# The first load of a decode kernel in two halves of 64 partitions, from two issuing engines

## The chip, the core and the metric

The kernel runs on one core of a Trainium2 chip. A core has four engines that compute (TensorE, VectorE, ScalarE, GpSimd), SyncE, which here issues transfers, and 16 DMA engines that carry data between the chip's main memory (HBM) and the core's on-chip memory of 128 partitions (SBUF). SyncE and ScalarE each have a queue of transfers of their own. The metric is the device time of one execution in microseconds (us); the kernel before takes 691.82 us, the median of three runs.

## What is computed

One decode step: attention of one token with grouped heads over a cache of 32,768 positions, and beside it a gated feed-forward block, mixed by a scalar gate. All in float32.

```python
Hq, Hkv, Sk, Dh, D, F = 32, 8, 32768, 128, 512, 1792
g = sigmoid((x * gate_w).sum(-1, keepdims=True))
q = (x @ wq).reshape(1, 1, Hq, Dh).transpose(0, 2, 1, 3)
scores = einsum("bhqd,bhkd->bhqk", q, repeat(k_cache, 4)) * Dh ** -0.5
o = einsum("bhqk,bhkd->bhqd", softmax(scores), repeat(v_cache, 4))
a = o.transpose(0, 2, 1, 3).reshape(1, 1, Hq * Dh) @ wo
b = (silu(x @ w1) * (x @ w3)) @ w2
out = g * a + (1 - g) * b
```

The caches are 8 heads of 16.8 MB each for k and for v, 268 MB of the 296 MB that are read. wq and wo have 8.39 MB each, w1, w3 and w2 3.67 MB each.

## The kernel before

Three buffers of 128 partitions by 16,384 floats, `ra`, `rb` and `rc`, 8.39 MB each, take all large transfers in turn. All of these are issued by SyncE, in one fixed order, written out by hand at lines 34 and 131 to 165; each issue is preceded by a wait on a semaphore that says that the buffer's last reader is done. Transfers of SyncE's queue are carried in the order of issue.

The start: lines 30 to 34 issue wq into `rc` (semaphore `l_q`), and w1 and w3 side by side into `rb` (`l_w1`, `l_w3`). For wq each of the 128 partitions takes four rows of the matrix, which follow each other in HBM: one run of 65,536 B. Then all engines meet at a barrier (line 38). SyncE goes on with the two halves of the first k tile into `ra` (131, 132), and then waits (133) until TensorE has done the second of two passes over `rb` (`c_e`) before it issues the next k tile into `rb` (134). ScalarE issues three small transfers from its own queue: x, 2 KB (168), gate_w, eight runs of 256 B (169), and zeros to the output (175). Both loads add to the semaphore `l_x`.

The first computation: VectorE (192, 194) and TensorE (200) wait for `l_x`. From x TensorE makes `xp`, x laid over the partitions, and a sum for the gate (209). At line 210 it waits for `l_q` and then multiplies by wq (215). VectorE transposes the result (227), ScalarE copies it in 16 pieces into `winraw` (231), and GpSimd puts it into the weights' window (271). TensorE meanwhile waits for w1 and w3 and does the two passes of the feed-forward block (247 to 250, in `ff_rows`, line 242); ScalarE (254) and VectorE (256 to 261) make of them the hidden row `htp`, which is kept to the end. ScalarE waits ahead of that for the zeros' landing (252).

The loop: for each of the eight heads VectorE transposes the k tiles in place (355), TensorE multiplies them by the query (284) and, a head later, v by the probabilities (298); ScalarE takes the exponentials. At the end wo comes into `rc` in two halves (434 waits for each), and w2 into `ra` in five pieces (441, 451).

Of the kernel before, what the change touches and what calls it, by code (L numbers as in the profile page):

```python
# [9 lines left out]
P = 128  # L10
# [14 lines left out]
@with_exitstack  # L25
def kernel(ctx, tc, x, k_cache, v_cache, wq, wo, w1, w3, w2, gate_w, out):
    nc = tc.nc
    rb, rc = (nc.alloc_sbuf_tensor(n, [P, 16384], F32).ap() for n in ("rb", "rc"))
    l_q, l_w1, l_w3 = (nc.alloc_semaphore(n) for n in ("l_q", "l_w1", "l_w3"))
    loads = [(rc, wq, l_q)]  # L30
    n = w1.shape[0] * w1.shape[1] // P
    loads += [(rb[:, i * n:(i + 1) * n], w, sem) for i, (w, sem) in enumerate(((w1, l_w1), (w3, l_w3)))]
    for to, w, sem in loads:
        i = nc.sync.dma_start(to, w.rearrange("(p c) n -> p (c n)", p=P)).then_inc(sem, 16)

        tc.no_tile_sem_insts.add(i.ins.name)
    tc.close()
    tc.compile()
    _program(nc, rb, rc, l_q, l_w1, l_w3, x, k_cache, v_cache, wq, wo, w1, w3, w2, gate_w, out)


def _program(nc, rb, rc, l_q, l_w1, l_w3, x, k_cache, v_cache, wq, wo, w1, w3, w2, gate_w, out):
    pe, dve, act, pool, sp = nc.tensor, nc.vector, nc.scalar, nc.gpsimd, nc.sync
# [119 lines left out]
    for i in range(2):  # L163
        e = slice(i * D // 2, (i + 1) * D // 2)
# [42 lines left out]
    dve.tensor_copy(xp[:, :, 0], mc[:, NC:2 * NC]).then_inc(t_x, 1)  # L207
    take(t_x, 2)
    n_gate = c_q.by(pe.matmul(mc[:, 0:1], ones[0:1], gsm[0:1], start=True, stop=True))
    pe.wait_ge(l_q, 16)  # L210
    for c in range(NC):
        for b in range(2):
            for j in range(4):
# [225 lines left out]
    for k in range(W2[1]):  # L439
        t = k % 4  # L440
        i = pe.matmul(  # L441
            acc[32 * t:32 * t + 32, :], htp[:, k, :], w2t[:, k, :], start=False, stop=(k >= W2[1] - 4),
            skip_group_check=True,
        )
# [65 lines left out]
```

## Time and profile before

| | us |
|---|---|
| median of three runs | 691.82 |
| lowest and highest run | 691.80, 691.91 |
| span of the profiled execution, first to last instruction | 690.5 |
| TensorE matmul busy in it | 380.2 (55%) |
| VectorE busy | 307.0 (44%) |
| ScalarE busy | 41.7 (6%) |

The profiled execution's own time is given as its span alone; the median lies 1.3 us above it. A span leaves out what lies ahead of the first instruction and behind the last.

A row of the timeline gives the start and the duration in us, the engine (a name that ends in q is the sequencer, which issues), the line, the operation, what is written and read, the count, and in brackets the idle time before it and what ended it. A row of the DMA issues gives what goes where, the issuing queue, the count, and the median time from issue to landing. The line of GB/s divides the span, or a window of it, into 40 equal slices and counts a packet's bytes in the slice in which it starts. Queue q1 is SyncE's, q10 ScalarE's.

### The profile page before, as it was taken

The page shows a single profiled execution, that of the slowest core. Times are in us where ns is not written, and L with a number is a line of the kernel's source. Part 1 is how long each engine was busy: PE and PEld are TensorE (multiplying, and loading weights), DVE is VectorE, ACT ScalarE, POOL GpSimd, SP SyncE. Part 2 cuts the span into 40 slices and gives each one's busy share as a digit, 9 for nine tenths or more (in the row PEclk, how much of TensorE's full clock was granted, in tenths as well). Part 3 has the DMA queues.
Part 4 walks back from the last instruction along what each step waited for, and adds up shares of the span by engine and source line. Part 5 has one row for each costly group of instructions (what it writes and reads, how often), then busy time and mean ns, then how long its engine had stood idle before and what let it go on. Part 6 is the DMA issues. An engine that isn't in the chain of part 4 may idle for free. (4 is left out here: it accounts for less than half of the span.)

```text
span 690.5 us, 6710 instructions
## 1 busy us (share of the span) xinstructions
PE 380.2 (55%) x2946; PEld 107.8 (16%) x2946; DVE 307.0 (44%) x194; ACT 41.7 (6%) x111; POOL 7.1 (1%) x41
## 2 busy tenths in 40 slices
PE   1737256466463744567563735457463734466567
PEld 1200011103010121103020211103010211103122
DVE  1019378291725537091725447091815446191000
ACT  0020011002000010002000010002000010002000
POOL 0000000000000000000000000000000000000000
PEclk9975587879685876768577967778676966768678
DMA  9999999999999999999999999999999999999997
GB/s 410 400 434 455 425 430 430 448 440 429 426 429 437 425 437 444 437 429 425 433 433 433 444 440 429 425 429 437 429 444 440 433 425 429 437 425 437 441 417 318
DMA packets 6222, 296.35 MB, mean 429 GB/s; under 512 B 707, under 2 KB 963, under 8 KB 1094
## 3 DMA queue, kind: packets, MB, share of 16 engines
q1 hardware_dynamic: 6192, 296.23, 99.3%
q8 instruction: 6, 0.10, 0.1%
q14 instruction: 2, 0.02, 0.0%
q10 hardware_dynamic: 22, 0.01, 0.0%
HBM read 296.23 MB, written 0.00 MB: 429 GB/s over the span
## 5 line engine op out<-in xcount | busy, mean ns | idle before, releaser
L355 DVE STREAM_TRANSPOSE rb<-rb 128x2048 f32<-128x2048 f32 x64 | 141.8, 2274 | 150.3 <-DVEq L125 150.3
L284 PE MATMUL psum<-rb,winbuf 128*32 128x512 f32 x512 | 96.7, 836 | 122.9 <-PEq L125 122.9
L355 DVE STREAM_TRANSPOSE ra<-ra 128x2048 f32<-128x2048 f32 x64 | 141.4, 2276 | 43.0 <-DVEq L125 43.0
L298 PE MATMUL psum<-rc,prob 128*32 128x512 f32 x896 | 112.8, 660 | 41.3 <-PEq L125 41.3
L284 PE MATMUL psum<-ra,winbuf 128*32 128x512 f32 x512 | 87.5, 782 | 83.8 <-PEq L125 83.8
L298 PEld LDWEIGHTS psum<-rc,prob 128*32 128x32 f32 x896 | 33.6, 121 | 117.0 <-issue 116.8
L379 DVE TENSOR_REDUCE mx<-psum 128x4 f32<-128x1024 f32 x8 | 9.8, 1225 | 82.7 <-DVEq L125 82.7
L284 PEld LDWEIGHTS psum<-rb,winbuf 128*32 128x32 f32 x512 | 13.5, 125 | 202.7 <-issue 202.7
L393 ACT COPY sbuf<-psum 128x512 f32<-128x512 f32 x16 | 9.9, 618 | 478.0 <-PE psum L284 478.0
L284 PEld LDWEIGHTS psum<-ra,winbuf 128*32 128x32 f32 x512 | 14.9, 122 | 149.3 <-issue 149.3
L399 ACT ACTIVATE prob<-psum,nm 128x256 f32<-128x256 f32 x32 | 18.9, 695 | 39.3 <-DVE nm L387 39.3
L308 PE MATMUL psum<-ident,sbuf 128*64 128x64 f32 x512 | 16.7, 223 | 0.8 <-PEq L125 0.8
L308 PEld LDWEIGHTS psum<-ident,sbuf 128*64 128x64 f32 x512 | 15.6, 138 | 7.6 <-issue 7.6
L360 DVE SCALAR_TENSOR_TENSOR otall<-psum,gate,recip 128x4 f32 (+1 forms) x8 | 1.7, 214 | 32.8 <-DVEq L125 32.8
L298 PE MATMUL psum<-rb,prob 128*32 128x512 f32 x64 | 8.5, 690 | 9.7 <-DMA rb<-in_A_v_cache_dram 9.7
L215 PE MATMUL psum<-rc,xp 128*32 128x512 f32 x64 | 9.8, 782 | 4.7 <-DMA rc<-in_A_wq_dram 4.7
L434 PE MATMUL psum<-rc,oq 128*32 128x512 f32 x64 | 10.7, 829 | 2.6 <-DMA rc<-in_A_wo_dram 2.2
L271 POOL COPY winbuf<-winraw 32x16 f32<-32x16 f32 x32 | 6.1, 191 | 535.4 <-PE psum L284 499.7
L242 PE MATMUL psum<-rb,xp 128*32 128x448 f32 x64 | 8.6, 690 | 5.4 <-DMA rb<-in_B_w_dram 5.4
L298 PE MATMUL psum<-ra,prob 128*32 128x512 f32 x64 | 9.6, 770 | 3.3 <-DMA ra<-in_A_v_cache_dram 3.3
L200 PE MATMUL psum<-ones,ob 1*128 1x1 f32 x8 | 2.0, 370 | 15.2 <-DMA prob<-in_gate_w_dram 15.2
L318 PE MATMUL psum<-fold,ob 128*128 128x4 f32 x64 | 8.4, 255 | 0.8 <-PEq L125 0.8
(62 smaller groups left out, 79.0 us busy)
## 6 DMA issues: line engine op xcount, KB each, us to landing
ra<-in_A_k_cache_dram SPq DMA_DIRECT2D x2, 4096.0 KB, 52.6
rc<-in_A_wo_dram SPq DMA_DIRECT2D x2, 4096.0 KB, 45.5
rb<-in_B_w_dram SPq DMA_DIRECT2D x2, 3584.0 KB, 34.7
ra<-in_B_w_dram SPq DMA_DIRECT2D x1, 1792.0 KB, 33.4
ra<-in_B_w_dram SPq DMA_DIRECT2D x1, 1024.0 KB, 35.5
ra<-in_B_w_dram SPq DMA_DIRECT2D x1, 512.0 KB, 36.3
ra<-in_B_w_dram SPq DMA_DIRECT2D x2, 128.0 KB, 36.0
rc<-in_A_v_cache_dram SPq DMA_DIRECT2D x14, 30.4
```

The source lines that it names most:

```text
L215: m = pe.matmul(pq[b][32 * j:32 * j + 32, :], xp[:, c, :], rc[:, o:o + REP * DH], start=(c == 0), stop=(c == NC - 1),)
L242: i = pe.matmul(ps[32 * j:32 * j + 32, 0:FJ], xp[:, c, :], rb[:, o:o + FJ], start=(c == 0), stop=(c == NC - 1))
L271: pool.tensor_copy(winbuf[32 * r:32 * r + 32, 16:144].rearrange("p (c k) -> p c k", k=32)[:, :, 4 * r:4 * r + REP], winraw[32 * r:32 * r + ...
L284: i = pe.matmul(s_ps[m][32 * g:32 * g + 32, :], winbuf[:, w:w + 32], region.rearrange("p (n c i) -> p c n i", c=4, i=32)[:, c, n:n + 16], ...
L298: i = pe.matmul(o_ps[32 * t:32 * t + 32, :], prob[:, w:w + 32], region[:, n * DH:(n + 4) * DH], start=(r == 0 and g == 0 and f == 0), stop ...
L308: i = pe.matmul(pf[64 * s:64 * s + 64, 64 * a:64 * a + 64], sbuf[:, a].rearrange("p i m -> p (i m)"), ident.rearrange("p (gf r s q) -> p s ...
L318: i = pe.matmul(mb[:, 0:REP], ob[:, b * P:(b + 1) * P], fold[:, 4 * b:4 * b + 4], start=(b == 0), stop=(b == 3))
L355: dve.transpose(part[:, c], part[:, c]).then_inc(t_tr, 1)
L379: dve.tensor_reduce(mx, pf.rearrange("p (a q) -> p q a", q=REP), axis=AX.X, op=ALU.max).then_inc(t_mx, 1)
L393: act.copy(sbuf[:, :, :, m], s_ps[m].rearrange("p (n i) -> p n i", i=32)).then_inc(t_ev, 1)
L399: act.activation(prob[:, 0:1024].rearrange("p (a n q) -> p n a q", a=16, q=REP)[:, :, :, q], pf.rearrange("p (n a q) -> p n a q", n=16, q= ...
L434: pe.matmul(acc[32 * t:32 * t + 32, :], oq[:, k:k + 32], rc[:, k * D:(k + 1) * D], start=(k < 4), stop=False, skip_group_check=True,)
```

## The change

The load of wq is cut by partitions. SyncE issues partitions 0 to 63, and ScalarE partitions 64 to 127, both ahead of the barrier. Each adds 16 to `l_q`, and TensorE waits for 32. The same bytes go to the same places; w1, w3 and all other transfers keep their engine and their order.

```diff
-    loads = [(rc, wq, l_q)]
     n = w1.shape[0] * w1.shape[1] // P
-    loads += [(rb[:, i * n:(i + 1) * n], w, sem) for i, (w, sem) in enumerate(((w1, l_w1), (w3, l_w3)))]
-    for to, w, sem in loads:
-        i = nc.sync.dma_start(to, w.rearrange("(p c) n -> p (c n)", p=P)).then_inc(sem, 16)
+    loads = [
+        (e, rc[h], wq.rearrange("(p c) n -> p (c n)", p=P)[h], l_q)
+        for e, h in ((nc.sync, slice(0, P // 2)), (nc.scalar, slice(P // 2, P)))
+    ]
+    loads += [
+        (nc.sync, rb[:, i * n:(i + 1) * n], w.rearrange("(p c) n -> p (c n)", p=P), sem)
+        for i, (w, sem) in enumerate(((w1, l_w1), (w3, l_w3)))
+    ]
+    for e, to, w, sem in loads:
+        i = e.dma_start(to, w).then_inc(sem, 16)
 
         tc.no_tile_sem_insts.add(i.ins.name)
...
     n_gate = c_q.by(pe.matmul(mc[:, 0:1], ones[0:1], gsm[0:1], start=True, stop=True))
-    pe.wait_ge(l_q, 16)
+    pe.wait_ge(l_q, 32)
```

The lines behind the change stand six further down in the new file. ScalarE's instructions from the start to its first computation, before (the branch at line 38 is the barrier, `ob` receives x and `prob` gate_w):

```order
L505 UNCONDITIONAL_BRANCH
L38 UNCONDITIONAL_BRANCH
L168 DMA ob<-in_A_x_dram 1x512
L169 DMA prob<-in_gate_w_dram 1x8x64
L175 DMA out_dram<-sbuf 1x512
L222 ACT_TABLE_LOAD
```

and with the change:

```order
L511 UNCONDITIONAL_BRANCH
L40 DMA rc<-in_A_wq_dram 64x16384
L44 UNCONDITIONAL_BRANCH
L174 DMA ob<-in_A_x_dram 1x512
L175 DMA prob<-in_gate_w_dram 1x8x64
L181 DMA out_dram<-sbuf 1x512
L228 ACT_TABLE_LOAD
```

The three small transfers, which were the first of ScalarE's queue, now stand behind half of wq in it. On SyncE the first row alone is another, 64 partitions for 128.

## The prediction

> **What bounds the kernel now.** I read the page first, then the chain of waits, then the first 80 us by the timeline. On the page:
>
> ```profile
> span 690.5 us, 6710 instructions
> DMA  9999999999999999999999999999999999999997
> GB/s 410 400 434 455 425 430 430 448 440 429 426 429 437 425 437 444 437 429 425 433 433 433 444 440 429 425 429 437 429 444 440 433 425 429 437 425 437 441 417 318
> q1 hardware_dynamic: 6192, 296.23, 99.3%
> ```
>
> The 16 DMA engines are busy in every slice, 99.3% of the span with SyncE's queue (q1) alone. No slice passes 455 GB/s, and most lie between 425 and 445. The end of the chain says the same:
>
> ```profile
> 672.29 5.34 PE psum L434 x32
> 677.63 2.14 another core or an unknown queue
> 679.82 5.34 PE psum L434 x32
> 685.16 1.71 PE psum L441 x14
> 686.87 1.87 PE psum L451 x60
> ```
>
> TensorE's last work stops for 2.14 us in the middle of line 434 until the second half of wo lands, and then runs to the end. So the end is set by when the stream of bytes is through, plus a tail of some 11 us (690.5 - 679.8) that the change does not touch. Computation matters only if it comes so late that a queue runs dry. The sum is therefore: what the change does to the time in which the first 8.39 MB arrive, and whether later issues still come before the queue is empty.
>
> **The stretch that is changed.** The timeline, in order of time:
>
> ```profile
> 0.73 0.37 SPq L34 DMA_DIRECT2D rc<-in_A_wq_dram  x1
> 1.16 0.90 SPq L34 DMA_DIRECT2D rb<-in_B_w_dram  x2
> 2.86 0.53 ACTq L168 DMA_DIRECT2D ob<-in_A_x_dram  x1
> 3.42 0.73 ACTq L169 DMA_DIRECT2D prob<-in_gate_w_dram  x1
> 15.21 0.68 DVE L192 TENSOR_TENSOR sbuf<-ob,prob 1x512 f32<-1x512 f32 x1 [10.96 <-DMA prob<-in_gate_w_dram]
> 17.60 0.55 PE L209 MATMUL psum<-gsm,ones 1*128 1x1 f32 x2 [0.35 <-PEq L125]
> 22.84 9.81 PE L215 MATMUL psum<-rc,xp 128*32 128x512 f32 x64 [4.68 <-DMA rc<-in_A_wq_dram]
> 32.47 3.18 PE L242 MATMUL psum<-rb,xp 128*32 128x448 f32 x32
> 41.06 5.37 PE L242 MATMUL psum<-rb,xp 128*32 128x448 f32 x32 [5.41 <-DMA rb<-in_B_w_dram]
> 46.50 0.33 SPq L134 DMA_DIRECT2D rb<-in_A_k_cache_dram  x1
> 50.85 8.89 DVE L355 STREAM_TRANSPOSE ra<-ra 128x2048 f32<-128x2048 f32 x4 [2.69 <-DVEq L125]
> 79.93 2.31 DVE L355 STREAM_TRANSPOSE rb<-rb 128x2048 f32<-128x2048 f32 x1 [10.46 <-DVEq L125]
> ```
>
> wq is issued at 0.73, and line 215, which waits for it, starts at 22.84. SyncE issues five transfers by 3.65, then waits for c_e until 46.50. How the engines carry it, in windows of two views (columns of the first two rows: stretch; its length; busy time and count of PE, PEld, DVE, ACT, POOL; clock; DMA share; GB/s. The others are the DMA view of 5 to 19 us, in 40 slices of 0.35 us):
>
> ```profile
> 22.00:42.00 20.00, 13.76 (x104) 3.70 (x108) 1.94 (x3) 4.43 (x17) 0.76 (x4) 0.92 1.01 433
> 100.00:650.00 550.00, 308.93 (x2455) 88.41 (x2454) 263.90 (x159) 32.43 (x86) 4.59 (x24) 0.75 1.00 433
> GB/s 1311 374 0 0 0 0 1317 1312 374 0 0 0 0 1502 1311 187 0 0 0 187 1686 936 187 0 0 0 187 1872 749 187 0 0 0 187 1878 936 0 0 0 0
> q1 hardware_dynamic: 89, 5.83, 96.1%
> q10 hardware_dynamic: 19, 0.01, 0.2%
> ```
>
> In full flow the rate is 433 GB/s, so one engine moves 433/16 = 27.1 GB/s. A packet of wq is one row of 65,536 B (5.83 MB over 89 packets, with 9 of these being tiny ones), so it takes 65,536/27.1 = 2.42 us. The slices count bytes at the packet's start: they show waves, two or three full slices and then four empty ones, about every 2.4 us. So all 16 engines begin a row within about 1 us of each other and go through their eight rows of wq nearly in step. The small packets of ScalarE's queue (q10) get in between.
>
> **The change, part by part.**
>
> *Issue.* SyncE issues 64 rows where it issued 128, ScalarE the other 64 beside it; SyncE's issues stay five. The row for 128 partitions is 0.37 us, so a gain or a loss is at most about 0.4 us at either end. ScalarE had nothing to do before the barrier (its first row is at 2.86, when SyncE also goes on). I take 0.
>
> *The rate of a half.* This is the term that decides, and no row shows a large transfer of fewer than 128 partitions. Before, 128 rows over 16 engines are 8 for each, and the 16 engines write all 128 partitions at once. After, each engine has four rows of the lower half and four of the upper, from two queues that take turns. As the engines run in step, all 16 are in the lower half at one time and then all in the upper: 16 engines into 64 partitions. If the 27.1 GB/s is the engine's own pace, nothing is lost: bound 0. If it is what a sixteenth of the partitions can take in, two engines now share each group, the half moves at 433/2 = 217 GB/s, and a row takes 4.84 us: 8 x 2.42 = 19.4 us lost, the other bound (691.8 and 711.2 for the whole). A gain is excluded, since no slice of the page goes over 455 GB/s. I take a value near the upper bound: for nothing to be lost the memory's side would need a spare of two, and no row here shows any above 455/433 = 1.05, nearest to none. From 19.4 something comes off. Two engines that share a group with an offset d lose 2.42 - d per row, not 2.42; the waves are at most three slices (1.05 us) wide for 16 engines, so the offsets of pairs lie between 0 and 1 us, and a load has landed only when its slowest pair has. With 0.15 us for that pair the loss is 8 x (2.42 - 0.15) = 18.2 us.
>
> [...]
>
> *x and gate_w behind a half.* They were first in ScalarE's queue and landed at 15.2, although issued by 3.42 + 0.73 = 4.15: a queue that alternates with 2.42 us rows gets one small packet through per row. Now they stand behind four rows of wq, so they arrive after wq. Behind them SyncE's queue carries w1 in rows of 28,672 B, 1.06 us each (28,672/27.1). Before, the last of them came 11.1 us after its issue (15.21 - 4.15), some five turns of 2.42; five turns of 1.06 are 5.3 us. From landing to the end of line 209 it was 18.15 - 15.21 = 2.9 us, so line 215 starts about 8.2 us after wq rather than with it. Its wait goes from l_q to l_x at lines 192 and 200. Queued behind on TensorE are lines 215 and 242, on ScalarE the copies of line 231, and SyncE waits at line 134 for the second pass of 242.
>
> Does that reach the stream? w3 lets the second pass begin at 41.06, the first having ended at 32.47 + 3.18 = 35.65: 5.4 us of the 8.2 vanish there. The rest, 2.8, reaches line 134, less what a warmer clock takes off the second pass (5.37 against 3.18): at most 2.8 us later than the stream. The cover is the queue: the transfer of line 134, issued at 46.50, is used at 79.93, 33.4 us later, of which 8.39 MB at 433 GB/s are 19.4. The row of the DMA issues that has nothing ahead of it in a queue,
>
> ```profile
> rc<-in_A_wq_dram SPq DMA_DIRECT2D x1, 22.1
> ```
>
> gives 22.1 us from issue to landing, so 2.7 beside the bytes. Line 134's transfer thus lay in the queue for 33.4 - 19.4 - 2.7 = 11.3 us. A delay of 2.8 us costs nothing; gone with that cover, it would cost itself. VectorE's line 261 would end at most 3 us later against the stream, where 2.69 us were idle, and its next wait for rb was 10.46 us long.
>
> *Semaphore.* Line 210 now waits for 32 on l_q, an increment more, no instruction more: 0.
>
> *Sum.* Profiled span 690.5 + 0 + 18.2 + 0 + 0 = 708.7. The runs' median, 691.82, stands 1.3 above that span, so 710.0.
>
> **Rivals.**
>
> *The engine's pace is the limit (not slower).* The engines stay 99% busy with the same bytes, the order alone changes, the late x and gate_w are hidden: 691.8, give or take the 0.4 of the issue. For it: on the page one queue fills all engines, whatever the rows' length. Against it: no row shows spare on the partitions' side. [...]
>
> *The engines fall out of step.* If half of them begin with ScalarE's rows, or drift, each side of the partitions is used at once. With pairs half a row apart the loss is 8 x 1.21 = 9.7 us: 701.5. For it: the two issues are simultaneous, so which queue an engine meets first is open, and starts spread over 1 us. Against it: the load waits for the slowest pair, and the waves hold from 5 to 19 us.
>
> *The cover fails.* x and gate_w need turns of a full shared row (4.84 us) each: 5 x 4.84 = 24.2 instead of 5.3, 18.9 more. Line 134 is then 2.8 + 18.9 = 21.7 late, 11.3 are covered, 10.4 are not: 710.0 + 10.4 = 720.4. Against it: by then SyncE's queue is at w1's shorter rows.
>
> *Faster.* The first rows arrive earlier. Slice one has 410 GB/s against 433 over 17.3 us: a gap of 0.9 us is all there is to win, so under 0.2%.
>
> **How the numbers follow.** Half rate in step 0.66 (705 to 713), out of step 0.13 (693.2 to 705), engine's pace 0.14 (690.5 to 693.2), cover fails 0.04 (above 713), a gain by something not seen 0.03. The likeliest one's own value is 710.0. A measurement of this kernel tells 0.2% (1.4 us) from no change: faster 0.03, within 0.14, slower 0.66 + 0.13 + 0.04 = 0.83. The range takes in the first two cases and a little above, 693.5 to 714, some 0.80.
>
> **What would show it.** *Rate:* the GB/s of the first slices near 217 for about 38 us, wq used at about 41 rather than 22.84, and w1, w3 and everything behind later by the same 18. If the first two slices still show 400 or more, the main step is wrong. *In step:* after the first 40 us the rate is 433 again and the loss stays constant to the end. *x and gate_w:* line 192 starts after wq has landed, and line 215 waits for it. *Cover:* no slice with a gap after 60 us, and line 434's wait near 2 us. A time under 693.2 would refute the half rate; one above 714, the cover.

## The result

The changed kernel takes 712.04 us, the median of four runs (712.02 to 712.18); the kernel before, beside it on the same chip, 691.87. The ratio is 1.0292, with a 95% interval of 1.028 to 1.0304: 20.2 us slower. The forecast was 710.0, in a range of 693.5 to 714.

The page of the changed kernel, the same lines as before:

```profile
span 710.6 us, 6711 instructions
DMA  9899999999999999999999999999999999999997
GB/s 236 177 343 434 457 421 436 436 428 439 432 428 446 424 428 446 424 428 450 421 428 454 417 428 454 417 428 454 417 428 457 421 421 457 428 421 450 428 412 328
q1 hardware_dynamic: 6128, 292.03, 96.6%
q10 hardware_dynamic: 102, 4.20, 2.8%
```

The span grew by 20.1 us, and all of it lies in the first three slices (17.8 us each): 236, 177 and 343 GB/s where there were 410, 400 and 434. (236 and 177 have a mean of 207; a slice counts the whole packet that starts in it.) From the fourth on the rate is what it was. The line of DMA shows next to nothing of it: the engines are "busy" at 9 or 8 tenths throughout, since a packet counts as busy for all the time that it takes, also when it takes twice as long. Bytes per time tell it, busy time does not.

The start in the timeline:

```profile
0.73 0.55 SPq L40 DMA_DIRECT2D rc<-in_A_wq_dram  x1
0.73 0.59 ACTq L40 DMA_DIRECT2D rc<-in_A_wq_dram  x1
3.16 0.33 SPq L137 DMA_DIRECT2D ra<-in_A_k_cache_dram  x1
47.09 0.68 DVE L198 TENSOR_TENSOR sbuf<-ob,prob 1x512 f32<-1x512 f32 x1 [42.52 <-DMA prob<-in_gate_w_dram]
49.97 8.51 PE L221 MATMUL psum<-rc,xp 128*32 128x512 f32 x64
58.31 6.19 PE L248 MATMUL psum<-rb,xp 128*32 128x448 f32 x64
64.56 0.33 SPq L140 DMA_DIRECT2D rb<-in_A_k_cache_dram  x1
70.82 8.89 DVE L361 STREAM_TRANSPOSE ra<-ra 128x2048 f32<-128x2048 f32 x4 [3.84 <-DVEq L131]
99.90 15.47 DVE L361 STREAM_TRANSPOSE rb<-rb 128x2048 f32<-128x2048 f32 x7 [10.46 <-DVEq L131]
```

The two issues start together and take 0.55 and 0.59 us for 64 rows each, longer than the 0.37 that one took for 128. The first transposition of `ra` starts at 70.82 (50.85 before), that of `rb` at 99.90 (79.93): 19.97 us later both. So the loss is complete before 70 us and is carried unchanged to the end. And how the engines carry wq, by the DMA issues, and by the DMA view of 5 to 19 us in 40 slices of 0.35 us:

```profile
rc<-in_A_wq_dram SPq DMA_DIRECT2D x1, 41.8
rc<-in_A_wq_dram ACTq DMA_DIRECT2D x1, 42.2
GB/s 0 0 0 0 0 1685 936 374 0 0 0 0 0 0 0 0 0 0 0 1685 936 374 0 0 0 0 0 0 0 0 0 0 0 1685 936 374 0 0 0 0
q10 hardware_dynamic: 32, 2.10, 70.3%
q1 hardware_dynamic: 16, 1.05, 35.1%
```

Three waves begin at slices 5, 19 and 33: 14 slices, 4.9 us, where it was 2.42. A wave is 16 packets, one row for each engine, and the queues alternate: 32 rows of q10 and 16 of q1 make two waves of ScalarE's half around one of SyncE's. It goes on so: each window of 5 us from 9 to 39 us (9 to 14, 14 to 19 and so on) holds 16 packets of one queue and none of the other, and these 16 fill 98.4% of the 16 engines' time in it. So all engines were in the same half at the same time.

### The profile page after: what moved, and what is told of

Same layout as the page of the kernel before. It is cut to its first block, busy times and chain, and to the rows that moved or that the text cites. A ratio compares the mean times of both kernels' runs of the same rounds, so it can differ in the third digit from the quotient of the medians.

```text
span 710.6 us, 6711 instructions
## 1 busy us (share of the span) xinstructions
PE 373.8 (53%) x2946; PEld 107.8 (15%) x2946; DVE 307.0 (43%) x194; ACT 41.7 (6%) x111; POOL 7.0 (1%) x41
## 5 line engine op out<-in xcount | busy, mean ns | idle before, releaser
L314 PE MATMUL psum<-ident,sbuf 128*64 128x64 f32 x512 | 18.3, 235 | 0.8 <-PEq L131 0.8
L314 PEld LDWEIGHTS psum<-ident,sbuf 128*64 128x64 f32 x512 | 17.2, 149 | 8.4 <-issue 8.4
L440 PE MATMUL psum<-rc,oq 128*32 128x512 f32 x64 | 7.3, 595 | 3.8 <-DMA rc<-in_A_wo_dram 3.4
L206 PEld LDWEIGHTS psum<-ones,ob 1*128 1x128 f32 x8 | 1.9, 322 | 47.1 <-DMA prob<-in_gate_w_dram 47.1
```

What stands on the lines that cost most here:

```text
L206: m = pe.matmul(mc[:, NC + c:NC + c + 1], xr.rearrange("o (p c) -> o c p", c=NC)[:, c], ones[0:1, 0:1], start=True, stop=True,)
L314: i = pe.matmul(pf[64 * s:64 * s + 64, 64 * a:64 * a + 64], sbuf[:, a].rearrange("p i m -> p (i m)"), ident.rearrange("p (gf r s q) -> p s ...
L440: pe.matmul(acc[32 * t:32 * t + 32, :], oq[:, k:k + 32], rc[:, k * D:(k + 1) * D], start=(k < 4), stop=False, skip_group_check=True,)
```

## The experiments

### What makes the halves slow: the two queues, the cut, or the late x

Three theories were open. The partitions' side takes in half as much when only half of the partitions is written; two queues on one engine cost time; or the late x and gate_w do. One run keeps the cut and takes one queue, another keeps the two queues and cuts by columns.

One queue:

```diff
-        for e, h in ((nc.sync, slice(0, P // 2)), (nc.scalar, slice(P // 2, P)))
+        for e, h in ((nc.sync, slice(0, P // 2)), (nc.sync, slice(P // 2, P)))
```

> Both halves of 64 partitions, but both issued by SyncE, one behind the other in one queue; ScalarE's queue has only the small transfers. Theory "partitions": what costs is that 16 engines write into 64 partitions at a time, so it takes as long as the change, a row of wq 4.9 us, the time 711 to 713. Rival "queues": what costs is that two queues take turns on each engine, so with one queue the rows take 2.42 us again and the time is 691.5 to 692.5. x and gate_w land early again under both (line 198 at about 15 to 30).

Two queues, cut by columns:

```diff
-        (e, rc[h], wq.rearrange("(p c) n -> p (c n)", p=P)[h], l_q)
-        for e, h in ((nc.sync, slice(0, P // 2)), (nc.scalar, slice(P // 2, P)))
+        (e, rc[:, h], wq.rearrange("(p c) n -> p (c n)", p=P)[:, h], l_q)
+        for e, h in ((nc.sync, slice(0, 8192)), (nc.scalar, slice(8192, 16384)))
```

> wq in two halves again, from SyncE and ScalarE at the same time, but cut by columns: each transfer has all 128 partitions and 8,192 columns. Theory "partitions": rows of 32,768 B take 1.21 us each, nothing is lost, 691.5 to 692.5, although x and gate_w stand behind half of wq in ScalarE's queue and line 221 starts some 7 us after wq. Rival "queues": the loss stays, 711 to 713. A third theory, that the late x and gate_w cost time by themselves, expects 694 to 700 here.

Measured: one queue 713.28 us (ratio 1.0309, 1.0292 to 1.0327); by columns 692.02 (1.0001, 0.9992 to 1.0011) against 691.92. One queue, timeline and DMA view of 5 to 19 us:

```profile
23.57 0.68 DVE L198 TENSOR_TENSOR sbuf<-ob,prob 1x512 f32<-1x512 f32 x1 [18.26 <-DMA prob<-in_gate_w_dram]
44.27 9.22 PE L221 MATMUL psum<-rc,xp 128*32 128x512 f32 x64 [17.75 <-DMA rc<-in_A_wq_dram]
GB/s 0 0 0 0 0 1685 749 374 187 0 0 0 0 0 0 0 0 0 0 563 1507 562 374 0 0 0 0 0 0 0 0 0 0 0 749 1498 562 187 0 0
```

By columns, timeline and windows:

```profile
26.68 0.68 DVE L198 TENSOR_TENSOR sbuf<-ob,prob 1x512 f32<-1x512 f32 x1 [22.43 <-DMA prob<-in_gate_w_dram]
29.55 9.90 PE L221 MATMUL psum<-rc,xp 128*32 128x512 f32 x64
45.54 0.33 SPq L140 DMA_DIRECT2D rb<-in_A_k_cache_dram  x1
2.00:22.00 20.00, 0.00 (x0) 0.00 (x0) 1.14 (x5) 1.28 (x1) 0.79 (x5) 1.00 0.98 419
```

With one queue x and gate_w are there at 23.57, line 221 waits for wq itself until 44.27, and the loss is whole. With two queues and all partitions the rate is 419 GB/s from 2 to 22 us and nothing is lost, although gate_w arrives at 26.68 and line 221 starts 6.7 us later than before (29.55 against 22.84). This takes away both rivals: neither the alternation of queues nor the late x costs time here. The loss belongs to the cut by partitions.

### Which partitions: their number, or fixed groups

Pieces of other sizes, all from SyncE. Of these edits and the ones below, only the added lines are shown; TensorE's wait for `l_q` (line 216 of the changed kernel) is set to 16 for each transfer that adds to it.

```diff
+        for e, h in ((nc.sync, slice(0, 32)), (nc.sync, slice(32, 96)), (nc.sync, slice(96, 128)))
```

> wq from SyncE alone in three pieces: partitions 0 to 31, 32 to 95, and 96 to 127. Theory "partitions", in the form that the intake counts by the number of partitions written at a time: the middle piece costs as a half does (16 engines into 64 partitions, 19.4 us for 4.19 MB), the outer ones twice that rate's price (into 32), 19.4 us for each: 58.2 instead of 19.4, so about 731. In the form that it counts by fixed groups, of which partitions 0 to 63 reach one half and 64 to 127 the other: the middle piece, which has 32 of each side, runs at the full rate, 2.42 us a row and 9.7 us in all, and the outer ones at half the rate, 9.7 us each: 29.1 instead of 19.4, so about 701.6. [...] Rival "queues": 691.5 to 692.5.

```diff
+        for e, h in ((nc.sync, slice(32 * i, 32 * i + 32)) for i in range(4))
```

> wq from SyncE alone in four pieces of 32 partitions. Intake by the number of partitions: each piece of 2.1 MB at a quarter of 433 GB/s, 19.4 us, 77.5 in all instead of 19.4: about 750. Intake by fixed groups, of which 0 to 31 and 32 to 63 reach the same half: a quarter goes at half the rate, just as the half does, 38.7 to 39.5 us in all: 711 to 713. Rival "queues": 691.5 to 692.5.

Measured: 702.46 us (1.0153, 1.0136 to 1.017) with the piece of 32 to 95, and 712.97 (1.0304, 1.0287 to 1.0321) with four quarters. Windows of the first, cut where its pieces change (the GB/s at the end):

```profile
11.50:21.50 10.00, 2.58 (x10) 2.44 (x10) 1.67 (x4) 0.17 (x1) 0.00 (x0) 1.00 1.00 414
21.50:31.50 10.00, 0.00 (x0) 0.00 (x0) 0.00 (x0) 0.00 (x0) 0.00 (x0) 1.00 0.99 210
```

Partitions 32 to 95 are 64 partitions and move at 414 GB/s; 96 to 127 move at 210. Four quarters cost no more than two halves. So the number of partitions does not decide: by that form these would be 731 and 750. The form with two fixed groups, 0 to 63 and 64 to 127, each with half of the rate, gave 701.6 and 711 to 713, and fits both. Within one group the rate is 206 to 214 GB/s (16 rows of 65,536 B in 5.1 or 4.9 us). The runs show the two groups alone, and nothing finer within a half.

### Destination or source

The middle piece also reads another place of HBM than the change's halves do. In the next run the middle partitions take the rows that the lower half of the change reads:

```diff
+        (nc.sync, rc[h], wq.rearrange("(p c) n -> p (c n)", p=P)[f], l_q)
+        for h, f in ((slice(0, 32), slice(64, 96)), (slice(32, 96), slice(0, 64)), (slice(96, 128), slice(96, 128)))
```

> The three pieces of partitions 0 to 31, 32 to 95 and 96 to 127 again, but the middle piece reads the rows of wq that the change's lower half reads (0 to 63), and the first piece reads rows 64 to 95; the rows land on other partitions, so what is computed is the query by a wq with its rows exchanged. Theory "destination": the middle piece is at the full rate because of the partitions that it writes, whatever it reads, 702 to 703 as with the rows in place. Rival "source": the half is slow because of the place in HBM that it reads, so the middle piece is now as slow as the change's half, 711 to 714.

702.47 us (1.0153, 1.0136 to 1.017), with these windows:

```profile
11.50:21.50 10.00, 2.57 (x10) 2.43 (x10) 1.67 (x4) 0.17 (x1) 0.00 (x0) 1.00 1.03 420
21.50:31.50 10.00, 0.00 (x0) 0.00 (x0) 0.00 (x0) 0.00 (x0) 0.00 (x0) 1.00 0.99 210
```

The source rows that took twice as long into partitions 0 to 63 go at 420 GB/s into 32 to 95. It is the destination.

### Whether engines that are out of step get the rate back

The forecast had a rival in which the engines fall out of step and use both halves at once. Two runs tried to bring that about with a tiny transfer ahead of the halves, of 8 rows, meant for 8 of the engines, or of 16:

```diff
+    loads.insert(0, (nc.sync, rb[0:8, 14336:14848], wq.rearrange("(p c) n -> p (c n)", p=P)[0:8, 0:512], l_q))
```

> The change, with one tiny transfer of SyncE ahead of it: 8 rows of 2 KB into unused columns of rb (it adds to l_q, which waits for 48). It changes nothing that is computed. If 8 rows go to 8 of the 16 engines, these 8 use up SyncE's first turn on it and begin with a row of ScalarE's half, while the other 8 begin with SyncE's half. Theory "in step": the loss comes from all engines being in one half at the same time; with the engines that share a group in different halves a row takes little over 2.42 us, the offset missing by some 0.3 us of a row, so 8 x 0.3 = 2.4 us are lost instead of 20 and the time is 693 to 699. Rival "halves are slow in themselves": a transfer of 64 partitions goes at half its rate whatever the other engines do: 711 to 713.

> The same with 16 rows of 2 KB ahead, one for each engine: all 16 engines use up SyncE's first turn, and all begin with ScalarE's half. Theory "in step": they are together again and the loss is whole, 711 to 713. If it is only the extra transfer as such that helps in the run with 8 rows, this one is as fast as that.

712.7 us (1.0299, 1.0282 to 1.0316) and 712.75 (1.0301, 1.0284 to 1.0319). With the 8 rows, the DMA view of 1.5 to 5 us has these counts:

```profile
q10 hardware_dynamic: 16, 1.05, 139.4%
q1 hardware_dynamic: 16, 0.02, 1.5%
```

All 16 engines began with a row of ScalarE's half (16 packets, 1.05 MB), and none with a large row of SyncE's: the tiny transfer pushed SyncE's half behind ScalarE's on every engine. The intended state was not reached, and the run tells nothing of it.

The next three put the halves into one queue, as 16 pieces of 2,048 columns in turn, with 8 rows of 8 KB ahead of them or not, and as 8 pieces of all partitions:

```diff
+        (nc.sync, rc[h, 2048 * i:2048 * i + 2048], wq.rearrange("(p c) n -> p (c n)", p=P)[h, 2048 * i:2048 * i + 2048], l_q)
+        for i in range(8) for h in (slice(0, P // 2), slice(P // 2, P))
...
+    loads.insert(0, (nc.sync, rb[0:8, 14336:16384], wq.rearrange("(p c) n -> p (c n)", p=P)[0:8, 0:2048], l_q))
```

> wq from SyncE's queue alone, in 16 pieces of 64 partitions by 2,048 columns, lower and upper half in turn, so each engine has four rows of 8 KB of the lower half, four of the upper, and so on. All engines begin together. Theory "in step": they are in the same half all the time, the loss is whole, 711 to 714. [...]

> The same 16 pieces, and ahead of them in the same queue a transfer of 8 rows of 8 KB into unused columns of rb; by the run with 8 rows of 2 KB it goes to 8 of the engines. These start with the first piece about as late as a piece takes at the full rate (1.2 us), so from then on they should be in one half while the other 8 are in the other. Theory "in step": each side of the partitions is written by 8 engines at a time, the rate is whole, 692.5 to 697. Rival "halves are slow in themselves": as without the 8 rows, 711 to 714.

> The same cut by columns with all 128 partitions, 8 pieces: what the short rows and the many issues cost by themselves. 691.5 to 693.5 under all theories; what it has above the kernel before is to be taken off the two others.

710.76 us (1.027, 1.0253 to 1.0288), 711.21 (1.0276, 1.0259 to 1.0293) and 692.24 (1.0004, 0.9995 to 1.0014). The short rows cost nothing by themselves; halves in short turns lose nearly all. With the 8 rows ahead the state was missed again, as the DMA view of 1.5 to 2.5 us (slices of 0.025 us) shows:

```profile
DMA packets 16, 0.07 MB, mean 66 GB/s; under 512 B 8, under 2 KB 8, under 8 KB 8
GB/s 0 0 0 0 0 0 0 0 655 983 328 0 0 0 0 0 0 0 0 328 328 0 0 0 0 0 0 0 0 0 0 0 0 0 0 0 0 0 0 0
```

The 8 rows and 8 packets under 512 B are all there is up to 2.5 us. The 16 take 21.6% of the 16 engines' time in this 1 us, so a row takes 0.43 us at most, and the last begins before 2.03. The first piece's rows come later, so the engines that carried the 8 rows were free again when these came.

The last two put four such transfers, of 8 rows as shown or of 16, behind the fourth of the 16 pieces, where the queue is deep:

```diff
+    loads[4:4] = [
+        (nc.sync, rb[8 * j:8 * j + 8, 14336:16384], wq.rearrange("(p c) n -> p (c n)", p=P)[8 * j:8 * j + 8, 0:2048], l_q)
+        for j in range(4)
+    ]
```

> The 16 pieces of 64 partitions by 2,048 columns in turn, and behind the fourth piece, where the queue is several pieces deep, four transfers of 8 rows of 8 KB each into unused columns of rb. Eight engines get four rows of 8 KB more, 1.2 us at the full rate, which is the time of a piece, so the other eight run a piece ahead from there on. Theory "in step": the first 4 pieces at half rate (some 5 us lost), the 12 behind at the whole rate, if the eight and the other eight are those that share groups: 697 to 700. Rival "halves are slow in themselves" (or the engines that share a group are on the same side of this cut): 711 to 713.

> The same with 16 rows in each of the four transfers, so that all 16 engines are held up alike and stay together. Both theories: the loss is whole and the extra rows cost 1 to 3 us, 711 to 715.

715.24 us (1.0338, 1.032 to 1.0355) and 714.45 (1.0323, 1.0306 to 1.034). The windows of the run with 8 rows, during and behind them:

```profile
12.00:18.00 6.00, 0.00 (x0) 0.00 (x0) 1.14 (x5) 1.28 (x1) 0.79 (x5) 1.00 1.00 160
18.00:24.00 6.00, 0.33 (x2) 0.33 (x2) 0.34 (x1) 0.00 (x0) 0.00 (x0) 1.00 1.03 230
24.00:30.00 6.00, 2.25 (x10) 2.10 (x9) 1.33 (x4) 0.17 (x1) 0.00 (x0) 1.00 1.01 225
```

The rows held engines up (160 GB/s), and afterwards the rate is 230 and 225, little more than without them (218 to 223 from 2 to 38 us in the run with the 16 pieces alone). No run shows the rate of both halves coming back. Which engines carried the 8 rows, and which engines write which of the 64 partitions, does not show in the trace. So it is open whether the rows parted the engines that, by the prediction's assumption, share a group, and by how much of a piece. The rival has no run for it and none that shuts it out.

## Why the prediction was right, step by step

**What bounds the kernel.** Right. The rate behind the third slice is the old one, and the 19.97 us at the first transpositions are the 20.1 of the span.

**Issue, taken as 0.** Small, but not nothing: two issues at once take 0.55 and 0.59 us, and the two halves of `ra` are issued at 3.16 instead of 2.84, some 0.3 us late.

**The rate of a half.** Right in its direction, and in that the partitions written set it: the runs show two fixed groups (414 GB/s into 32 to 95, 210 into 96 to 127). That two engines share a sixteenth of the partitions was the author's assumption, and no run shows it. The size was off by 2.0 us (18.2 forecast, 20.2 measured), and the term that was mis-sized is the row's time: 4.84 less 0.15 for the pair's offset, 4.69 us. It measured 4.92: from 24 to 39 us the DMA view has 48 rows in 98.4% of the 16 engines' time. The first row of each engine is a case of its own. It took 3.01 us before (16 packets from 1.6 to 4 us, at a share of 125.3%), where the prediction had 2.42 for all eight, and 4.83 with the change. So the rows lose 1.8 + 7 x 2.50 = 19.3 us, 1.1 more than forecast; they begin some 0.3 us later; and the remaining half a microsecond of the 20.1 is not placed.

Rows of the same half one after the other take still longer: with one queue, which gives an engine four of them, the waves begin at slices 5, about 19.5 and 34, some 5.1 us apart, and that run is 1.24 us slower than the change (713.28 - 712.04). Alternating halves gains a little on that. This is the direction of the offset's credit, but no run shows that the offset is what gains it. The doubled row of 4.84, which set the upper bound of 19.4, was itself too short.

**A misreading without effect.** The prediction took nine of the 89 packets of q1 from 5 to 19 us for tiny ones. 89 x 65,536 B are the 5.83 MB, so all 89 are rows of wq, and the tiny ones are q10's. The sum does not use it.

**x and gate_w behind a half.** Right that they come after wq (landed at 0.73 + 42.2 = 42.9, line 198 at 47.09) and that line 221 then waits for them: 7.1 us after wq, 8.2 forecast. The cut by columns shows by itself that this costs nothing (692.02 against 691.92).

**The cover.** Right, with more to spare. Line 140 was forecast up to 2.8 us late against the stream, and is 64.56 - 46.50 = 18.1 us later, so some 2 us early against it:

```profile
44.00:62.00 18.00, 14.54 (x114) 5.88 (x118) 2.99 (x6) 2.17 (x10) 0.00 (x0) 1.00 1.03 440
```

TensorE had all it needed once it began, worked without a stop and at the full clock (1.00), and made line 248's two passes in 6.19 us, against 3.18, a wait of 5.41 and 5.37 before (that last at a clock of 0.59, from 41 to 46.5 us). The transfer of line 140 was used at 99.90, and `rb` was waited for as long as before, 10.46 us.

**Rivals.** That the engines fall out of step did not happen, as the windows of one queue each show. That the engine's own pace is the limit is refuted by the piece of 32 to 95 beside the halves (414 GB/s against 206 to 214). That the cover fails did not happen, and there was no gain.

## What to carry to other kernels

Where DMA bounds a kernel as it does this one (99.3% of the span), cut a large load by columns and not by partitions into 0 to 63 and 64 to 127: the first is free here (692.02 against 691.92), the second nearly doubles the load's time from issue to landing, from 22.1 us to 42.2 with ScalarE issuing one half; with SyncE issuing both, TensorE waited for the load until 44.27 us. Where only 64 partitions are needed, 32 to 95 carried nearly the full rate here (414 GB/s, against 210 for the change's halves from 24 to 39 us). And look for such a loss in the bytes per slice, not in the DMA engines' busy share, which stayed at 8 or 9 tenths.

## What was not expected

A row that goes into a half takes more than twice as long: 65,536 B in about 5.1 us with one queue and 4.9 with two, against 2.42 with all partitions. What takes the part beyond twice is not shown. The issue of a half takes longer than that of the whole: 0.55 and 0.59 us for 64 rows each, 0.37 for 128. It is not that two sequencers issue at the same time, since by columns they do so in 0.37 and 0.41:

```profile
0.73 0.41 ACTq L40 DMA_DIRECT2D rc<-in_A_wq_dram  x1
0.73 0.37 SPq L40 DMA_DIRECT2D rc<-in_A_wq_dram  x1
```

The cut by partitions costs issue time as well; why is not shown.
